# Window attention with expert routing on one core: keys loaded whole and spread by copies, ranking by half a comparison, and a tabled order of work

## The chip, the cores and the metric

The kernel runs on one core of one Trainium2 chip. The metric is the device time of one execution in microseconds (us). All inputs lie in HBM, in a layout that the host prepared, and the eight results (one for each batch entry) go back to HBM.

## What is computed

There are 8 batch entries, 8 heads, 576 positions and 64 features in a head. Heads 0 to 3 attend to a plain window of the last 32 positions; heads 4 to 7 attend to every fourth position of the last 128. The attention output of a batch entry, 576 rows of 512, is then the input of an expert layer, in which only the 128 rows with the highest gate score go through a two-layer network.

```python
scores = scale * np.matmul(q, k.transpose(0, 1, 3, 2))
scores = np.where(masks[None, :, :, :], scores, -1000000000.0)
scores = scores - np.max(scores, axis=-1, keepdims=True)
attn = np.exp(scores)
attn = attn / (np.sum(attn, axis=-1, keepdims=True) + 1e-09)
x = np.matmul(attn, v)            # then heads side by side: (B, S, 512)
...
scores = np.einsum('bsd,d->bs', x, w_gate)
for b in range(B):
    top_idx = np.argpartition(-scores[b], capacity)[:capacity]   # capacity = 128
    h = np.maximum(x[b, top_idx] @ w1, 0.0)                       # 512 -> 1024
    ye = h @ w2                                                   # 1024 -> 512
    g = 1.0 / (1.0 + np.exp(-scores[b, top_idx]))
    out[b, top_idx] = x[b, top_idx] + g[:, None] * ye
```

All of it is float32. The two products of the expert layer are made of three float32r products each (high part by high part, and the two mixed ones).

## The kernel before

**Units.** The attention of a batch entry is cut into five units: two of plain windows (`p`, 256 positions each), one of the last 64 positions of both kinds (`l`), and two of dilated windows (`d`). A unit goes through `scores` (line 275, TensorE; in the first `masked=20` units the mask is added by further products, line 270), `maximum` (line 287, VectorE; later units use line 294, which adds the mask and takes the maximum), `subtract` (line 303), `transposes` (line 314, TensorE), `weights` (line 342, exponentials on ScalarE), `attend` (line 356, TensorE), `normalise` (lines 369 and 371), `divide` (line 379 on VectorE, or line 385 on ScalarE), `store` (lines 394 to 404, DMAs on SyncE's queue) and `gate` (line 418, the gate score of each row). There are three score tiles in PSUM, one tile for `attend`, and three tiles `m` for everything else.

**Keys.** The score product takes two heads at once: 128 rows of the contraction hold the 64 features of two heads, and the key tile `ks` has two planes, in each of which the rows of the other head are zero. `load_k` (line 215) writes the keys of each half straight into its plane, so it issues two DMAs of 288 KB for each kind of window; `load_q` (line 208) issues one of 576 KB. There is one buffer for each kind: the next batch entry's keys may only be loaded when the scores that read the old ones are done. `load_vp` (line 221) loads rows 0 to 63 and 96 to 127 of a value table, in two DMAs; the exponentials of a `p` unit go to places in three pieces, and four tiles `pt` serve five units.

**Routing.** After the five units of an entry, `split_scores` (lines 450 to 453), `order` (lines 462 and 466, 15 small products), `total` (line 471), `spread` (line 477) and `gather_scores` (lines 483, 484) bring the scores of all 576 positions to every partition. `rank` (line 492) then compares each of five tiles of 128 positions with all 576 and counts; `mark` (line 499) makes a one-hot tile of the slots, `pick` (line 507) turns it into row numbers, `number` (line 513) makes them integers, and `fetch` (line 521) gathers the chosen rows from the result in HBM by an indirect DMA on GpSimd.

**Expert layer.** `gate_dot` (line 544) makes the gate score of the chosen rows anew, lines 549 to 554 the sigmoid, `turn_x` (line 559) turns the rows, `split_hi` and `split_lo` (lines 527, 530) split them, `ffn1` (line 598) and `ffn2` (line 624) are 24 products of 512 columns each, `result` (line 629) adds, and `put` (line 635) scatters the rows to HBM. The 16 weight blocks of 256 KB are loaded by `load_weights` (line 430), rounded on ScalarE (line 438), and their rests are made on GpSimd (line 442).

**What sets the order.** Nothing is written out by hand. Each step is an operation in `Planner`, with an engine, a cost, the operations that it needs, buffers that it takes and frees, and a due time. `run` simulates the engines: of the operations that could start within 0.05 us of the earliest on an engine, it takes the one with the lowest due time, plus a penalty when TensorE would change its tiling. The order found is the order in which the program issues. Every engine's queue is then worked strictly in that order. The planner takes DMAs to move `RATE = 0.29` KB per ns. SyncE issues each DMA as soon as its buffer is free, however many are under way. While TensorE would idle in the first 50 us, products on a spare tile fill the gap (line 837).

```python
first = min(t for t, _ in cands)
t, w = min((c for c in cands if c[0] <= first + 0.05),
           key=lambda c: (c[1].due + (self.penalty if c[1].mode not in (None, mode) else 0.0), c[1].n))
```

Of the kernel before, what the change touches and what calls it, by code (L numbers as in the profile page):

```python
# [19 lines left out]
P = 128  # L20
# [19 lines left out]
    unit=3,  # L40
    gate=14.47,
    unit0=2.82, gate0=5.68, route0=8.95, ffn0=17.53,
    route=13.4,
    ffn=14.64,
    piece=0.89,
    switch=3,
    w1=12.51, w2=25.55, each=2,
    first=4.62, early=15.02, lead=13.59,
# [3 lines left out]
    rest=16,  # L52
    split=(1, 2, 3, 4, 5, 6),
    aq=(),
    masked=20,
    xv=5,
    xe=20,
)


class Work:


    def __init__(self, n, eng, cost, fn, deps, due, mode, takes, frees, lag, size, after, port):
        self.n, self.eng, self.cost, self.fn, self.due, self.mode = n, eng, cost, fn, due, mode
        self.deps, self.takes, self.frees = [d for d in deps if d is not None], list(takes), list(frees)
        self.lag, self.size, self.after, self.port = lag, size, after, port
        self.start, self.end, self.fill = None, None, 0


class Planner:
# [4 lines left out]
    RATE = 0.29  # L76
    LAND = 2.0

    def __init__(self, bufs, switch, fill, free):
        self.ops, self.bufs, self.penalty, self.fill, self.free = [], bufs, switch, fill, dict(free)  # L80

    def add(self, eng, cost, fn, deps=(), due=0.0, mode=None, takes=(), frees=(), lag=0.0, size=None, after=0.0, port=False):
        w = Work(len(self.ops), eng, cost, fn, deps, due, mode, takes, frees, lag, size, after, port)
        self.ops.append(w)
        return w

    def run(self):
        users, left, ready, order = {}, {}, {}, []
        free, mode, moved, port = self.free, None, 0.0, {"DVE": 0.0, "POOL": 0.0}
# [14 lines left out]
        for _ in self.ops:  # L104
            best = None
            for eng, ws in ready.items():
                cands = []
                for t, w in ws:
                    t = max(t, free.get(eng, 0.0))
# [31 lines left out]
            if w.size is not None:  # L141
                moved = max(moved, t + 1.0) + w.size / self.RATE / 1000
                w.lag = max(w.lag, self.LAND, moved - w.end + 0.5)
# [21 lines left out]
def tile_window_attention_moe(ctx, tc, qt, kt, va, vb, w_gate, w1, w2, masks, mask_l, ident, slots, toks, outs, capacity):  # L165
# [8 lines left out]
    pl = Planner(dict(BUFS, **{f"oh{i}": 1 for i in range(nt)}), T["switch"], T["fill"], dict(PE=5.0, DVE=5.5, ACT=3.0, POOL=T["zeros"], SP=0.8))  # L174
# [9 lines left out]
    thr_sb = cp.tile([P, 2 * 512 + HB], F32, name="thr_sb")  # L184
    wg = cp.tile([P, DM], F32, name="wg")
    slots_sb = cp.tile([P, max(nt, 1) * P], F32, name="slots_sb")
    toks32 = cp.tile([P, NTOK], F32, name="toks32")
    toks_sb = cp.tile([P, NTOK], F16, name="toks_sb")
    qs = [cp.tile([P, 2, S + 16 * i], F32, name=f"qs{i}") for i in range(2)]
    ks = [cp.tile([P, 2, 2, G + S], F32, name=f"ks{i}") for i in range(2)]  # L190
    vp = cp.tile([3 * G, 8, VW], F32, name="vp")
    vd = cp.tile([P, 4, VW], F32, name="vd")
    vl = cp.tile([P, 3, VW], F32, name="vl")
    pts = [cp.tile([P, 4, 4, 2, G], F32, name=f"pt{i}") for i in range(4)]
# [7 lines left out]
    ohs = [cp.tile([P, NTOK, P], F16, name=f"oh{i}") for i in range(max(nt, 1))]  # L202
# [4 lines left out]
    def load_q(b, kind, lo=0, hi=S):  # L207
        nc.sync.dma_start(out=qs[kind][:, :, lo:hi], in_=qt[b, kind].rearrange("d (p s) -> d p s", p=2)[:, :, lo:hi])
# [10 lines left out]
    def load_vp(b, lo=0, hi=8):  # L219
        for k, src in ((slice(0, GK), slice(0, GK)), (slice(GK, 3 * G), slice(3 * G, P))):  # L220
            nc.sync.dma_start(out=vp[k, lo:hi].rearrange("k c f -> k (c f)"),
                              in_=va[b, src, (4 + lo) * VW:(4 + hi) * VW])

    def load_vd(b):
        nc.sync.dma_start(out=vd.rearrange("k r f -> k (r f)"), in_=va[b, :, 0:4 * VW])

    def load_vl(b):
        for i in range(2):
            nc.sync.dma_start(out=vl[GK * i:GK * i + LK, 0:2].rearrange("k e f -> k (e f)"),
                              in_=vb[b, LK * i:LK * (i + 1)])  # L230
        nc.sync.dma_start(out=vl[:, 2], in_=va[b, :, 12 * VW:13 * VW])
# [31 lines left out]
    def scores(g):  # L263
# [3 lines left out]
        for c, (nw, rows) in enumerate(chunks(kind)):  # L267
# [4 lines left out]
            for p in range(2):  # L272
                for w in range(nw):
                    q, q0, k, k0 = window(kind, s, c, w)
                    nc.tensor.matmul(st[G * w:G * (w + 1), c, p], q[:, p, q0:q0 + G], k[:, p, :, k0:k0 + GK],  # L275
# [32 lines left out]
    def transposes(g):  # L308
# [11 lines left out]
        ("p", 0): (((0, GK, 0),), ((G, G, 0), (GK, G, G))),  # L320
        ("l", 0): (((0, GK, 0),), ((GK, GK, 0),)),
        ("d", 0): (((3 * G, G, 0),), ((GK, GK, 0),)),
    }
    PLACES["p", 1] = PLACES["d", 1] = PLACES["p", 0]

    def held(g):
        b, u = divmod(g, NU)
        return pts[{0: b % 2, 1: 1 - b % 2, 2: 2, 3: 3, 4: b % 2}[u]]
# [17 lines left out]
    def attend(g):  # L346
# [3 lines left out]
        n = 3 * G if kind == "p" or (kind, s) == ("d", 1) else P  # L350
# [37 lines left out]
    def store(g):  # L388
# [3 lines left out]
        eng = nc.scalar if kind in T["aq"] else nc.sync  # L392
        if kind == "p":
            eng.dma_start(out=o[256 * s:256 * (s + 1), 0:256].rearrange("(c q) f -> q c f", c=2), in_=x)
        elif kind == "d":
            for r in range(2):
                for j in range(2 * s, 2 * s + 2):
                    i = HB * r + G * (3 - j if s else j)
                    eng.dma_start(out=o[P * j:P * (j + 1), 256:512].rearrange("(n c r) f -> r n c f", c=2, r=2)[r],
                                      in_=x[i:i + G])  # L400
        else:
            eng.dma_start(out=o[4 * P:S, 0:256], in_=x[0:HB, 1])
            for r in range(DIL):
                eng.dma_start(out=o[4 * P:S, 256:512].rearrange("(n r) f -> r n f", r=DIL)[r],
                                  in_=x[G * r:G * r + 16, 0])


    def gate(g):
        b, (kind, s) = g // NU, UNITS[g % NU]
        if b not in sts:  # L410
            sts[b] = {n: wk.tile([P, NTOK], F32, tag=n, name=f"{n}_{b}") for n in ("sd", "sc", "rk")}
            sts[b]["sw"] = sws[b % 2]
# [11 lines left out]
    def load_weights(i):  # L424
# [5 lines left out]
        nc.sync.dma_start(out=raw[i], in_=src)  # L430
# [13 lines left out]


    def split_scores(b, by_vector):
        st, eng = sts[b], nc.vector if by_vector else nc.gpsimd
        sp = st["sp"] = wk.tile([P, 3, NTOK], BF16, tag="sp", bufs=2, name=f"sp_{b}")
        rest = wk.tile([P, NTOK], F32, tag="rest", bufs=2, name=f"rest_{b}")
        eng.tensor_copy(sp[:, 0], st["sd"])  # L450
        eng.tensor_tensor(out=rest, in0=st["sd"], in1=sp[:, 0], op=ALU.subtract)
        eng.tensor_copy(sp[:, 1], rest)
        eng.tensor_tensor(out=sp[:, 2], in0=rest, in1=sp[:, 1], op=ALU.subtract)

    def order(b):
        st = sts[b]
        pg = st["pg"] = ps.tile([P, 512], F32, tag="m", bufs=BUFS["m"], name=f"pg_{b}")
        sp = st["sp"]
        for c in range(2):
            for e in range(2):  # L460
                for i in range(3):
                    nc.tensor.matmul(pg[:, c:4 - c:3 - 2 * c], perm[:, c, e],
                                     sp[:, i, 0:4].rearrange("q (s c) -> q c s", s=2)[:, e],
                                     start=e == 0 and i == 0, stop=e == 1 and i == 2)
        for i in range(3):
            nc.tensor.matmul(pg[:, 4:5], perml, sp[:, i, 4:5], start=i == 0, stop=i == 2)
# [450 lines left out]
```

## Time and profile before

| | us |
|---|---|
| median of 3 runs (lowest, highest) | 272.23 (271.6, 272.88) |
| the profiled execution's own time | 272.17 |
| its span, first to last instruction | 270.5 |
| TensorE busy | 240.9 (89%) |
| VectorE busy | 203.0 (75%) |
| ScalarE busy | 143.5 (53%) |
| GpSimd busy | 56.2 (21%) |
| bytes moved by DMA | 51.04 MB, mean 189 GB/s |

The profile is of one execution. "PE" is TensorE's products, "PEld" its weight loads, "DVE" VectorE, "ACT" ScalarE, "POOL" GpSimd, "SP" SyncE; "L275" is line 275. A group's row has the line, engine and operation, output and inputs with their shapes, the count, then the busy time in us and the mean of one in ns, then the idle time before them and what ended it. A row of the table of stretches has its bounds, its length, the busy time and count of each engine, TensorE's granted clock, the share of the 16 DMA engines and the GB/s. A row of the chain of waits has a start, a length and what it was.

### The profile page before, as it was taken

What the parts mean: (1) busy time and instruction counts of PE and PEld (TensorE: products, weight loads), DVE (VectorE), ACT (ScalarE), POOL (GpSimd) and SP (SyncE); (2) the same over time, 40 slices, a digit from 0 to 9 for tenths busy, and PEclk for the clock granted to TensorE, in tenths of its full rate; (3) what the DMA queues carried; (4) which work ended last, traced back from release to release, by engine and by line L of the source; (5) the groups of instructions that cost most, each with busy time, mean ns of one, the idle gap of its engine ahead of it and who ended that gap; (6) DMA issues with size and microseconds to landing.
All of it is one profiled execution on the core that took longest, in us unless ns stands there. A gap on an engine that the chain in (4) does not pass through costs nothing.

```text
span 270.5 us, 9035 instructions
## 1 busy us (share of the span) xinstructions
PE 240.9 (89%) x3469; PEld 194.0 (72%) x3475; DVE 203.0 (75%) x893; ACT 143.5 (53%) x418; POOL 56.2 (21%) x92
## 2 busy tenths in 40 slices
PE   6759859884997887999999999999999999999892
PEld 1439647673985875888888788788888878777671
DVE  4327885999597595999899989978899798684221
ACT  2062718328292255655585797578577948522120
POOL 8922103250430326101110111101110101011101
PEclk9997997999799799999999999999999999999998
DMA  6999984989879994998599689738994430321101
GB/s 157 257 238 255 284 242 102 299 210 247 240 175 249 239 302 123 315 282 180 150 252 283 194 256 303 219 83 219 286 230 122 138 120 21 88 69 42 39 0 39
DMA packets 28732, 51.04 MB, mean 189 GB/s; under 512 B 4529, under 2 KB 16049, under 8 KB 28017
## 3 DMA queue, kind: packets, MB, share of 16 engines
q1 hardware_dynamic: 26976, 46.16, 64.0%
q0 software_dynamic: 1280, 4.20, 4.7%
q8 instruction: 27, 0.44, 0.7%
q10 hardware_dynamic: 432, 0.11, 0.2%
q14 instruction: 17, 0.13, 0.2%
HBM read 38.92 MB, written 11.53 MB: 187 GB/s over the span
## 4 chain that ended last, share of the span: by engine, by line
PE 51%; DMA 13%; DVE 13%; issue 13%; SPq 5%; ACT 2%; POOL 1%; POOLq 1%; DVEq 0%; ACTq 0%
PE a L356 12%; PE py L624 10%; PE s L275 10%; DMA ks<-in_kt_dram 9%; PE ph L598 9%; PE s L314 5%; DMA raw<-in_w_dram 4%; DVE junk L492 3%; DVE junk L418 2%; DVE mx L287 2%; DVE ms L303 2%; DVE x L379 2%; PE pht L609 2%; ACT pt L342 2%; SPq L215 1%
## 5 line engine op out<-in xcount | busy, mean ns | idle before, releaser
L342 ACT ACTIVATE pt<-s 32x256 f32<-32x256 f32 (+2 forms) x208 | 76.8, 369 | 35.4 <-PE s L314 27.2
L275 PE MATMUL s<-ks,qs 128*32 128x128 f32 x1216 | 46.8, 288 | 7.1 <-DMA ks<-in_kt_dram 7.1
L275 PEld LDWEIGHTS s<-ks,qs 128*32 128x32 f32 x1216 | 38.5, 115 | 9.0 <-issue 5.8
L418 DVE CUSTOM_DVE_ANT_0 junk<-x,wg 128x256 bf16<-128x256 f32 x80 | 38.8, 486 | 5.7 <-ACT x L385 2.6
L492 DVE SCALAR_TENSOR_TENSOR junk<-sb,sc,thr_sb 128x576 bf16<-128x576 f32 (+1 forms) x40 | 32.4, 811 | 0.9 <-ACT sb L484 0.9
L385 ACT ACTIVATE x<-a,rin 128x64 f32<-128x64 f32 (+1 forms) x128 | 27.9, 328 | 9.7 <-DVE rin L371 6.3
L314 PE MATMUL s<-id,ms 128*128 128x128 f32 x160 | 25.0, 282 | 3.5 <-issue 2.7
L624 PE MATMUL py<-w2h,hh 128*128 128x512 f32 x64 | 27.4, 428 | 0.5 <-ACT w2h L438 0.5
L598 PE MATMUL ph<-w1h,xh 128*128 128x512 f32 x64 | 27.1, 424 | 0.7 <-ACT xh L527 0.7
L624 PE MATMUL py<-w2l,hh 128*128 128x512 f32 x64 | 25.4, 398 | 0.8 <-POOL w2l L442 0.8
L598 PE MATMUL ph<-w1h,xl 128*128 128x512 f32 x64 | 25.4, 397 | 0.0
L624 PE MATMUL py<-w2h,hl 128*128 128x512 f32 x64 | 25.3, 395 | 0.0
L598 PE MATMUL ph<-w1l,xh 128*128 128x512 f32 x64 | 25.2, 394 | 0.0
L314 PEld LDWEIGHTS s<-id,ms 128*128 128x128 f32 x160 | 18.3, 142 | 8.5 <-issue 3.6
L287 DVE TENSOR_REDUCE mx<-s 128x8 f32<-128x512 f32 (+2 forms) x24 | 13.9, 591 | 13.6 <-PE s L275 13.6
L294 DVE CUSTOM_DVE_ANT_0 ms<-s,mk 128x64 f32<-128x64 f32 (+1 forms) x144 | 22.2, 215 | 0.0
L356 PEld LDWEIGHTS a<-vp,pt 96*64 96x64 f32 x512 | 17.0, 142 | 6.5 <-ACT pt L342 4.6
L521 POOL DMA_INDIRECT xe<-out_dram,ix x8 | 7.9, 990 | 65.5 <-DMA vl<-in_va_dram 21.8
L356 PE MATMUL a<-vp,pt 96*64 96x65 f32 x512 | 19.3, 230 | 2.3 <-ACT pt L342 2.3
L356 PEld LDWEIGHTS a<-vd,pt 96*64 96x64 f32 (+1 forms) x512 | 16.3, 137 | 6.6 <-ACT pt L342 3.5
L356 PE MATMUL a<-vd,pt 96*64 96x65 f32 (+1 forms) x512 | 18.4, 224 | 2.3 <-ACT pt L342 1.2
L635 POOL DMA_INDIRECT out_dram<-y,ix x8 | 8.5, 1062 | 44.0 <-DVE y L629 19.9
(96 smaller groups left out, 398.0 us busy)
## 6 DMA issues: line engine op xcount, KB each, us to landing
qs<-in_qt_dram SPq DMA_DIRECT2D x15, 576.0 KB, 4.4
ks<-in_kt_dram SPq DMA_DIRECT2D x30, 288.0 KB, 9.8
out_dram<-x SPq DMA_DIRECT2D x72, 64.0 KB, 3.6
vd<-in_va_dram SPq DMA_DIRECT2D x8, 520.0 KB
raw<-in_w_dram SPq DMA_DIRECT2D x16, 256.0 KB, 3.8
out_dram<-x SPq DMA_DIRECT2D x16, 256.0 KB
vp<-in_va_dram SPq DMA_DIRECT2D x7, 520.0 KB, 11.3
vp<-in_va_dram SPq DMA_DIRECT2D x9, 260.0 KB
```

Source lines behind the costliest of these rows:

```text
L275: nc.tensor.matmul(st[G * w:G * (w + 1), c, p], q[:, p, q0:q0 + G], k[:, p, :, k0:k0 + GK], start=not by_products(g), stop=p == 1 or not b ...
L287: nc.vector.tensor_reduce(out=mx[:n, lo:hi].rearrange("q c p h -> q (c p h)"), in_=st[:n, lo:hi].rearrange("q c p h k -> q (c p h) k"), ax ...
L294: nc.vector.tensor_tensor_reduce(out=ms[:rows, c, p, h], in0=st[:rows, c, p, h], in1=mask_of(g, c)[:rows], scale=1.0, scalar=-3.0e38, op0= ...
L314: nc.tensor.transpose(tt[:, p, c], dt[:, c, p].rearrange("q h k -> q (h k)"), id32)
L342: nc.scalar.activation(held(g)[to:to + size, 2 * h:2 * h + 2, 0:n, u], src, AF.Exp, scale=SCALE)
L356: nc.tensor.matmul(at[HB * (y % 2):HB * (y % 2 + 1), c, f], held(g)[:n, h, y].rearrange("k u q -> k (u q)"), v[:n, f], start=True, stop=True)
L385: nc.scalar.activation(x[:n, c, h, :], av[:n, c, h, 0:D], AF.Copy, scale=rin[:n, c, h:h + 1])
L418: nc.vector.tensor_tensor_reduce(out=junk[:n], in0=x[:n, c].rearrange("q h d -> q (h d)"), in1=wg[:n, 256 * dil:256 * (dil + 1)], scale=UP ...
L492: nc.vector.scalar_tensor_tensor(out=junk[:n], in0=st["sb"][:n], scalar=st["sc"][:n, t:t + 1], in1=thr_sb[:n, o:o + S], op0=ALU.subtract, ...
L598: nc.tensor.matmul(e["ph", n], e[x][:, i, 0:P], w[:, i, n * 512:(n + 1) * 512], start=i == 0 and j == 0, stop=i == 3 and j == 2)
L624: nc.tensor.matmul(e["py", j], e[x][:, i, j * P:(j + 1) * P], w[:, i, :], start=i == 0 and n == 0, stop=i == 7 and n == 2)
L635: nc.gpsimd.indirect_dma_start(out=outs[b][:, :], out_offset=bass.IndirectOffsetOnAxis(ap=ix[:m, 0:1], axis=0), in_=e["y", j][:m], in_offs ...
```

## The change

**Keys.** `load_k` loads a kind's keys in one DMA of 576 KB into a new tile `kin`; `spread_k` copies each half to its plane of `ks`, with two ScalarE copies of 64 rows by 1152 columns. A new load of `kin` waits for the copies of the entry before; the copies wait for the scores that read the planes. `load_vp` loads all 128 rows in one DMA (1040 KB in place of about 780), the exponentials of a `p` unit are in two pieces, not three, and each of five units has a tile `pt` of its own.

**Ranking.** `rank` compares tile t only with the positions from its own on (576, 448, 320, 192 and 64 columns) and keeps the comparisons; `count` adds the missing ones by ten small products with a column of -1, and `ranks` joins both. `mark` is one operation of 640 columns. `order` has 5 products in place of 15, and `total` sums their three parts. `pick` also carries the three parts of each score (`split_sums`, on GpSimd), so that `number` has the chosen scores, and `gate_dot` is gone. The tables of slots and rows are made on GpSimd and no longer loaded.

**Transfers.** Every plain DMA goes through `move`. One on SyncE waits until the latest transfer that has at least 1200 KB issued behind it has landed. The planner models this and takes 370 KB per us.

**Order.** A table `RANKS` has one number for each operation. Where its length equals the number of operations, the numbers take the place of all due times, and the tiling penalty is zero. The due times' parameters change too; of these `w1`, `early` and `lead`, which bound when loads may start, still act, as do `masked=18`, `xv=2` and `xe=15` (which units mask by products and which divide on VectorE: 28 of 40 units in place of 24) and `rest=12` (four weight rests on VectorE).

```diff
-    def load_k(b, kind, lo=0, hi=S):
-        o = 0 if kind else G
-        src = kt[b, kind].rearrange("d (p s) -> d p s", p=2)
-        for h in range(2):
-            r = slice(h * D, (h + 1) * D)
-            nc.sync.dma_start(out=ks[kind][r, :, h, o + lo:o + hi], in_=src[r, :, lo:hi])
+    moves = []
+
+    def move(out, in_, kb, eng=None):
+        i = (eng or nc.sync).dma_start(out=out, in_=in_).ins
+        behind = 0
+        for j, size, calm in reversed(moves):
+            if eng is None and (behind >= T["under"] or calm):
+                tc.add_manual_dep(i, j.name, mybir.DependencyInfo(mybir.DependencyClass.Sync, mybir.DependencyReason.DATA),
+                                  reason="not too many transfers")
+                break
+            behind += size
+        moves.append((i, kb, False))
...
+    def load_k(b, kind):
+        move(kin[kind], kt[b, kind], 576)
+
+    def spread_k(b, kind, h, eng):
+        o, r = 0 if kind else G, slice(h * D, (h + 1) * D)
+        out = ks[kind][r, h, o:o + 2 * S]
+        eng.copy(out, kin[kind][r]) if eng is nc.scalar else eng.tensor_copy(out, kin[kind][r])
...
     def load_vp(b, lo=0, hi=8):
-        for k, src in ((slice(0, GK), slice(0, GK)), (slice(GK, 3 * G), slice(3 * G, P))):
-            nc.sync.dma_start(out=vp[k, lo:hi].rearrange("k c f -> k (c f)"),
-                              in_=va[b, src, (4 + lo) * VW:(4 + hi) * VW])
+        move(vp[:, lo:hi].rearrange("k c f -> k (c f)"), va[b, :, (4 + lo) * VW:(4 + hi) * VW], 130 * (hi - lo))
...
     def rank(b, t):
         st = sts[b]
-        n = P if t < 4 else HB
-        junk = wk.tile([P, S], BF16, tag="junk2", bufs=1, name=f"junk2_{b}_{t}")
-        o = 512 - t * P
+        n, o = P if t < 4 else HB, t * P
         nc.vector.scalar_tensor_tensor(
-            out=junk[:n], in0=st["sb"][:n], scalar=st["sc"][:n, t:t + 1], in1=thr_sb[:n, o:o + S],
+            out=cm[t][:n, 0:S - o], in0=st["sb"][:n, o:S], scalar=st["sc"][:n, t:t + 1], in1=thr_sb[:n, 0:S - o],
             op0=ALU.subtract, op1=ALU.is_gt, accum_out=st["rk"][:n, t:t + 1])
 
-    def mark(b, s, t):
+    def count(b):
+        pr = sts[b]["pr"] = ps.tile([P, 512], F32, tag="m", bufs=BUFS["m"], name=f"pr_{b}")
+        for t in range(1, NTOK):
+            for i in range(t):
+                nc.tensor.matmul(pr[:, t:t + 1], cm[i][:, (t - i) * P:(t - i + 1) * P], less, start=i == 0, stop=i == t - 1)
+
+    def ranks(b):
         st = sts[b]
-        n = P if t < 4 else HB
-        nc.vector.tensor_scalar(
-            out=ohs[s][:n, t, :], in0=slots_sb[:n, s * P:(s + 1) * P], scalar1=st["rk"][:n, t:t + 1],
-            scalar2=None, op0=ALU.is_equal)
+        rk = st["rk"][:, 1:NTOK]
+        nc.vector.tensor_tensor(out=rk, in0=st.pop("pr")[:, 1:NTOK], in1=rk, op=ALU.add)
+
+    def mark(b, s):
+        nc.vector.tensor_tensor(out=ohs[s], in0=slots_sb[:, s], in1=sts[b]["rk"].unsqueeze(2).to_broadcast([P, NTOK, P]),
+                                op=ALU.is_equal)
...
+    found = [int(r) for r in RANKS.split()]
+    if len(found) == len(pl.ops):
+        pl.penalty = 0.0
+        for w, r in zip(pl.ops, found):
+            w.due = r
     for i, w in enumerate(pl.run()):
```

More of the change, by code (lines that the diff above doesn't have):

```diff
@@ L39 @@
     warm=9,
[L40 to L48, printed above, removed]
+    unit=3.89,
+    gate=8.95,
+    unit0=1.86, gate0=-16.79, route0=8.14, ffn0=20,
+    route=1.69,
+    ffn=25.91,
+    piece=1.07,
+    switch=2.69,
+    w1=24.88, w2=34.11, each=0.86,
+    first=10, early=17.8, lead=15,
     fill=(50.0, 0.7),
@@ L51, with __init__ @@
     groups=(1,),
-    rest=16,
+    rest=12,
     split=(1, 2, 3, 4, 5, 6),
[L54 to L57, printed above, removed]
-)
+    spread=("ACT", "ACT"),
+    calm=(),
+    under=1200,
+    masked=18,
+    xv=2,
+    xe=15,
+)
+RANKS = """
[33 rows of a table added]
+"""
 class Work:
-    def __init__(self, n, eng, cost, fn, deps, due, mode, takes, frees, lag, size, after, port):
+    def __init__(self, n, eng, cost, fn, deps, due, mode, takes, frees, lag, size, after, port, calm):
         self.n, self.eng, self.cost, self.fn, self.due, self.mode = n, eng, cost, fn, due, mode
         self.deps, self.takes, self.frees = [d for d in deps if d is not None], list(takes), list(frees)
-        self.lag, self.size, self.after, self.port = lag, size, after, port
+        self.lag, self.size, self.after, self.port, self.calm = lag, size, after, port, calm
         self.start, self.end, self.fill = None, None, 0
@@ L88, in run @@
         users, left, ready, order = {}, {}, {}, []
-        free, mode, moved, port = self.free, None, 0.0, {"DVE": 0.0, "POOL": 0.0}
+        free, mode, moved, port, moves = self.free, None, 0.0, {"DVE": 0.0, "POOL": 0.0}, []
         pools = {t: [[0.0] * n, 0, {}] for t, n in self.bufs.items()}
@@ L104, in run @@
         for _ in self.ops:
-            best = None
+            best, under, clear = None, 0.0, 0.0
+            for size, end, calm in reversed(moves):
+                if under >= self.under or calm:
+                    clear = end
+                    break
+                under += size
             for eng, ws in ready.items():
@@ L173, in tile_window_attention_moe @@
     BUFS = dict(s=3, a=1, m=3, ms=3, x=4, xe=2 * nt + 2, raw=4, e=1)
-    pl = Planner(dict(BUFS, **{f"oh{i}": 1 for i in range(nt)}), T["switch"], T["fill"], dict(PE=5.0, DVE=5.5, ACT=3.0, POOL=T["zeros"], SP=0.8))
+    pl = Planner(dict(BUFS, **{f"oh{i}": 1 for i in range(nt)}), T["switch"], T["fill"], T["under"], dict(PE=5.0, DVE=5.5, ACT=3.0, POOL=T["zeros"], SP=0.8))
     id32 = cp.tile([P, P], F32, name="id32")
@@ L429, in load_weights @@
             src = w2[(i - 8) * P:(i - 7) * P, :]
-        nc.sync.dma_start(out=raw[i], in_=src)
+        move(raw[i], src, 256)
     def parts(i):
@@ new lines, in tile_window_attention_moe @@
+        o = ranked[b] = [A("DVE", 0.06 + 0.0013 * (S - P * t), lambda b=b, t=t: rank(b, t), [o] + counts[-1:], d + 1 + 0.5 * t, port=True) for t in range(NTOK)]
+        counts.append(A("PE", 0.3, lambda b=b: count(b), o, d + 4, mode=128, takes=[("m", ("pr", b))], lag=0.1))
+        o = A("DVE", 0.12, lambda b=b: ranks(b), counts[-1:] + ([picks[b - 2]] if b > 1 else []), d + 4, frees=[("m", ("pr", b))])
+        marks = [A("DVE", 0.75, lambda b=b, i=i: mark(b, i), [o], d + 4, port=True, takes=[(f"oh{i}", b)]) for i in range(nt)]
```

278 lines of the change are left out of this document (149 added, 129 removed), and 33 rows, old and new, of the table RANKS.

## The prediction

> **What bounds the kernel now.** I read the page's busy line first, then a table of stretches that I cut where the work changes its nature, and then the chain of waits inside the stretches that lose time.
>
> ```profile
> PE 240.9 (89%) x3469; PEld 194.0 (72%) x3475; DVE 203.0 (75%) x893; ACT 143.5 (53%) x418; POOL 56.2 (21%) x92
> GB/s 157 257 238 255 284 242 102 299 210 247 240 175 249 239 302 123 315 282 180 150 252 283 194 256 303 219 83 219 286 230 122 138 120 21 88 69 42 39 0 39
> ```
> ```profile
> 0.00:20.00 20.00, 12.25 (x158) 6.80 (x162) 7.17 (x16) 6.00 (x14) 13.80 (x35) 0.99 0.89 217
> 20.00:78.50 58.50, 48.94 (x966) 39.87 (x962) 47.76 (x139) 29.68 (x75) 16.26 (x17) 0.92 0.85 228
> 78.50:107.80 29.30, 24.60 (x327) 19.90 (x326) 21.39 (x65) 12.43 (x29) 7.89 (x9) 0.94 0.85 227
> 107.80:227.00 119.20, 118.90 (x1794) 99.00 (x1792) 108.03 (x616) 82.27 (x265) 13.41 (x27) 1.00 0.75 207
> 227.00:270.50 43.50, 36.24 (x241) 28.40 (x237) 18.70 (x59) 13.15 (x38) 4.87 (x5) 0.98 0.15 46
> ```
> ```profile
> 0.00:107.80 107.80, 85.79 (x1440) 66.58 (x1447) 76.31 (x219) 48.12 (x117) 37.95 (x61) 0.94 0.86 226
> ```
>
> From 107.8 to 227 us TensorE is busy 118.9 of 119.2 us at full clock: that stage is bound by TensorE, and nothing that is done for another engine there can shorten it. Before 107.8 us it is busy 85.8 of 107.8, at a clock of 0.94, and part of that busy time is spare products. In the same stretch the DMA engines are busy at 0.86 and move 226 GB/s. So the stage that can give something is the first one. The cut at 107.8 us is where the second entry's chosen rows are turned for its expert layer; the first entry's expert layer has just ended. The chain shows what that point waited for:
>
> ```profile
> 2.18 4.62 DMA ks<-in_kt_dram
> 9.92 9.38 DMA ks<-in_kt_dram
> 83.13 10.30 DMA ks<-in_kt_dram
> 93.49 8.20 DMA raw<-in_w_dram
> 102.55 2.63 DMA raw<-in_w_dram
> 105.89 1.28 POOL w2l L442
> 107.95 0.44 PE px L559 x4
> ```
> ```profile
> qs<-in_qt_dram SPq DMA_DIRECT2D x15, 576.0 KB, 4.4
> ks<-in_kt_dram SPq DMA_DIRECT2D x30, 288.0 KB, 9.8
> raw<-in_w_dram SPq DMA_DIRECT2D x16, 256.0 KB, 3.8
> ```
>
> Keys and weights stand in the chain for 4.62 + 9.38 + 10.30 + 8.20 + 2.63 = 35.1 us. A key transfer of 288 KB takes 9.8 us to land where a query transfer twice its size takes 4.4: it stands behind what was issued earlier and not needed as soon.
>
> **The change, stage by stage.** I count what must be done up to the same cut (the turning of the second entry's rows), for each resource that could set it, and take the rest of the program from the trace.
>
> *How much work lies before the cut.* I laid the tabled ranks over the operations: counting the operations of the new program by hand gives 962, as many as the table has, so the table is used. In that order the cut comes after the 15th attention unit (the fifth of the third entry). In the trace of before it comes after 16. The new program thus owes one more unit after the cut. Its price on TensorE:
>
> ```profile
> 158.14 1.88 PE s L275 x64
> 157.06 1.08 PE a L356 x32
> 154.38 0.59 PE s L314 x4
> 154.97 2.09 PE py L624 x9
> ```
>
> The first row is the scores of two units, 0.94 each; with 0.59 for the transposes and 1.08 for the attending products a unit is 2.61 us.
>
> *DMA up to the cut.* By the tabled order SyncE has issued, when the last weight block goes out: queries, keys and values of three entries (3 x 4190 KB), the gate row (256), queries and keys of one kind of the fourth entry (1152), 16 weight blocks (4096) and eleven units' results (2560). That is 20,634 KB, and with the first entry's gathered rows (256) 21.4 MB. At 226 GB/s this takes 94.7 us, at 226/0.86 = 263 (all engines busy) 81.4, and 1.5 us lie ahead of the first packet. The larger value table is in it (208 KB more for an entry, 0.6 MB here, 2.5 us at 250 GB/s). What speaks for a higher rate: fewer, whole transfers (the 30 key DMAs of the row above become 15), and keys that can be fetched while the planes are still read, because the new tile takes them; in before a key load sat behind the scores. I take 250 GB/s, 0.95 of the full rate: 85.6 + 1.5 = 87 us.
>
> *VectorE up to the cut.*
>
> ```profile
> L287 DVE TENSOR_REDUCE mx<-s 128x8 f32<-128x512 f32 x16 | 10.9, 680 | 7.1 <-PE s L275 7.1
> L303 DVE TENSOR_TENSOR ms<-s,mx 128x512 f32<-128x512 f32 x16 | 11.0, 690 | 2.1 <-POOL ms L715 1.5
> L369 DVE TENSOR_SCALAR den<-a 128x8 f32<-128x8 f32 x32 | 5.2, 161 | 9.5 <-PE a L356 8.9 <-PE pg L466 0.3
> L371 DVE RECIPROCAL rin<-den 128x8 f32<-128x8 f32 x32 | 6.5, 203 | 1.1
> L379 DVE TENSOR_TENSOR x<-a,rin 128x512 f32<-128x512 f32 x20 | 13.8, 689 | 1.0 <-DMA out_dram<-x 0.2
> L418 DVE CUSTOM_DVE_ANT_0 junk<-x,wg 128x256 bf16<-128x256 f32 x72 | 35.5, 493 | 5.2 <-ACT x L385 2.6 <-ACT h L604 0.2 <-ACT sb L484 0.2
> L492 DVE SCALAR_TENSOR_TENSOR junk<-sb,sc,thr_sb 128x576 bf16<-128x576 f32 x32 | 26.1, 814 | 0.9 <-ACT sb L484 0.9
> L499 DVE TENSOR_SCALAR oh<-slots_sb,rk 128x128 f16<-128x128 f32 x32 | 9.1, 285 | 1.1
> ```
>
> The L287 to L418 rows, the last of them twice, make 3.41 us for a unit; 15 units are 51.1. Routing an entry was 5 x (0.814 + 0.285) = 5.5. Now the comparisons have 1600 columns, not 2880: between 2.26 us (all by width) and 4.07 (nothing by width), and I take 2.5, near the first, as five rows of 576 columns are mostly width. The one marking operation of 640 columns is taken at 0.90, by width from the L492 row, and four further small ones at the L369 to L371 rows, 0.7. That is 4.1, so 1.4 us less for an entry, 8.2 for two. The first expert layer has four splits or sums and four weight rests at about 0.69 (the L379 row), 5.5. The sum is 65 us. It can start when the first scores are there, at about 11 us: 76 us if VectorE never waits. TensorE needs less: 15 x 2.61 + 48 x 0.232 (2.09/9) + some 4 for routing and masks = 54 us from 10 us on.
>
> *Start.* The first scores come later. Two whole transfers, 1.18 MB, must land (5.4 us at the 217 GB/s of the first row, from 1.5 on, and about 0.6 to signal: 7.5), and then two copies must run:
>
> ```profile
> L483 ACT COPY sb<-pa 128x512 f32<-128x512 f32 x8 | 4.7, 588 | 5.9 <-PE pa L477 5.9
> L484 ACT COPY sb<-pa 128x64 f32<-128x64 f32 x8 | 1.8, 221 | 0.0
> ```
>
> By these two rows a column is 0.82 ns, so 1152 columns cost 1.11 us; the bounds are 0.59 (the 512-column row) and 1.32 (that row by width alone). The first score is at 7.5 + 2.2 = 9.7 us, against 6.8 where the first key transfer ended. But the third unit, which needs both kinds, needs 2.89 MB in the new order of loads, 13.3 + 1.5 = 15 us, against 19.3 (9.92 + 9.38). So the stage starts 3 us later and is 4 us ahead after two units; the DMA term above already has this.
>
> *The cut and the end.* The cut moves from 107.8 to 87 by the largest of the three terms, DMA, 20.8 us. One unit is owed, 2.6. The stage behind the cut keeps its 162.7 us if nothing there becomes late: span 270.5 - 20.8 + 2.6 = 252.3. The execution's own time is 272.17 against a span of 270.5, 1.7 around it, and 272.17 is 0.06 below the median. Forecast: 254.0 us.
>
> *Does something become late behind the cut?* The rows for ScalarE and what leaves VectorE:
>
> ```profile
> L342 ACT ACTIVATE pt<-s 32x256 f32<-32x256 f32 x112 | 42.0, 375 | 4.2 <-PE s L314 1.8
> L385 ACT ACTIVATE x<-a,rin 128x64 f32<-128x64 f32 x112 | 24.8, 330 | 9.7 <-DVE rin L371 6.3 <-PE s L275 1.3 <-DMA out_dram<-x 1.0
> L544 DVE CUSTOM_DVE_ANT_0 junk<-xe,wg 128x512 bf16<-128x512 f32 x8 | 5.4, 680 | 1.7 <-DMA xe<-out_dram,ix 1.7
> L294 DVE CUSTOM_DVE_ANT_0 ms<-s,mk 128x64 f32<-128x64 f32 x128 | 19.6, 216 | 0.0
> L442 POOL TENSOR_TENSOR w2l<-raw,w2h 128x512 fp32r<-128x512 f32 x8 | 10.2, 1280 | 22.4 <-ACT w2h L438 22.3
> ```
>
> ScalarE gains 32 copies (35.5 us), loses two of six exponentials in each of 16 units (32 x 0.375 = 12.0) and four units' divisions (32 x 0.330 = 10.6): 143.5 + 13 = 156.5 us. Even if 10 us of that fell between 107.8 and 227, it would be 92 of 119. VectorE loses 8 x 1.4 for routing and 8 x 0.68 for the gate score, gains four divisions (2.8), four rests (2.7) and two units masked there (each 8 x 0.216 in place of 0.68, 1.0): about 9 us less. GpSimd loses four rests (5.1) and gains a split of four small operations for each entry. TensorE saves 10 of 15 small products and gains 10: nothing. With TensorE at 118.9 of 119.2, all this is covered there. The cover goes if a copy is late: it stands in ScalarE's queue ahead of a unit's exponentials, and TensorE's next attending product would wait, at 2.2 us for a pair.
>
> **The rivals.**
>
> *The same bytes at the same rate (chance 0.20).* The DMA engines were already busy at 0.86, and the change moves no byte less. Then the cut is at 94.7 + 1.5 = 96.2, the span 270.5 - 11.6 + 2.6 = 261.5, the time 263. For it: three stretches in a row with 217 to 228 GB/s, whatever was computed. Against it: slices at 284 to 315, so the mean is not the ceiling.
>
> *VectorE is the bound (0.20).* If bytes arrive in time throughout, the cut is at 76 and the time 270.5 - 31.8 + 2.6 + 1.7 = 243. Against it: in the 20-to-78.5 row VectorE is busy only 47.8 of 58.5.
>
> *The hold on transfers starves the core: slower (0.10).* SyncE now waits until an earlier transfer has landed, and everything behind stands in its queue: results, which the gathers wait for, and the next loads. The price can be worked out. All loads (37,872 KB) and the results of about seven entries (8064), 47.0 MB, must have moved some 43 us before the end (the last entry's units end there in the trace, the 227.00 row). So 273.6 us, the edge of "slower", asks for 47.0/(273.6 - 1.7 - 43) = 205 GB/s; below that the kernel is slower. With 1.23 MB under way this is a landing time of 6.0 us. At 186 GB/s (6.6 us) the time would be 253 + 43 + 1.7 = 298. The query row, 576 KB in 4.4 us amid other transfers, speaks against it; the key row, 9.8, speaks for it, but that is backlog which the hold itself removes. [...]
>
> *The plan does not fit the chip: no change (0.05).* Every queue is worked in the planned order, and the planner now takes 370 KB per us. The best slice of the page is 315 GB/s. Where a product is queued ahead of one whose data is there, its wait comes back; if the 20.8 us come back that way, the time is near 272. [...]
>
> **How the numbers follow.** The forecast has 0.45. Rivals: 0.20 at 263, 0.20 at 243, 0.10 slower, 0.05 no change. About 0.5% (1.4 us) is what can be told from no change, so faster 0.85, same 0.05, slower 0.10. The range goes from 243 (VectorE) to 267 (the first rival and one more late unit and copy, 2.6 + 1.5); it leaves out the slower case, the unchanged one and a little below.
>
> **What would show it.** First scores near 9.7 us and the third unit's near 15; the second entry's rows turned near 87 us, 15 units before it; DMA near 250 GB/s up to there; TensorE without gaps behind; key transfers gone from the chain but for the first; 32 copies near 1.1 us. The sum is wrong if that turn is not early, or if it is early and the stage behind it is longer than 165 us.

## The result and the profile after

The kernel after took 260.5 us (257.65 to 260.88, 4 runs) against 272.12 us (271.6 to 272.88, 4 runs) before: a ratio of 0.955, with a 95% interval of 0.948 to 0.962. The forecast was 254.0 us with a range of 243 to 267, so the time lies inside the range, but the gain is 11.6 us where 18.1 were forecast. The profiled execution took 260.74 us, with a span of 259.0. The times of the runs are medians of all executions, while the ratios leave out those that took over 1.5% longer than their kernel's fastest; the profiles of two experiments below, the column halves and the hold of 600 KB, are of such slow executions.

The busy line, the GB/s of the 40 slices and the packets of the page:

```profile
PE 236.3 (91%) x3442; PEld 186.4 (72%) x3442; DVE 194.3 (75%) x918; ACT 160.9 (62%) x386; POOL 60.9 (24%) x149
...
GB/s 209 339 329 346 309 151 283 345 324 199 314 214 353 272 232 361 206 259 232 124 273 230 191 257 322 168 157 197 273 127 177 72 17 101 73 39 40 43 0 40
DMA packets 24571, 53.10 MB, mean 205 GB/s; under 512 B 3920, under 2 KB 14288, under 8 KB 23632
```

More bytes are moved (53.1 against 51.0 MB), and the slices of the first third now lie mostly between 280 and 360 GB/s, where before they lay around 240. The table of stretches, cut at the same event as in the prediction (the turning of the second entry's rows, line 635 here, at 85.64 us) and at the last attending product (222.2 us; before it was at 231.5):

```profile
0.00:85.60 85.60, 74.15 (x1318) 55.74 (x1319) 69.15 (x207) 56.48 (x112) 36.89 (x91) 1.00 0.87 287
...
85.60:222.20 136.60, 133.65 (x1955) 109.00 (x1954) 112.26 (x674) 97.67 (x261) 19.20 (x50) 1.00 0.64 199
222.20:259.00 36.80, 28.53 (x174) 21.61 (x173) 12.91 (x39) 6.70 (x13) 4.82 (x8) 0.99 0.12 38
```
```profile
107.80:231.50 123.70, 123.40 (x1844) 102.59 (x1842) 110.80 (x629) 86.68 (x280) 14.38 (x28) 1.00 0.74 203
231.50:270.50 39.00, 31.74 (x190) 24.80 (x189) 15.93 (x47) 8.74 (x23) 3.91 (x4) 0.98 0.13 41
```

The second fence is the kernel before, cut at the same events. Up to the cut 22.2 us were gained (107.8 to 85.6). Behind it 10.7 us were given back (162.7 to 173.4): the middle stretch grew from 123.7 to 136.6 us, and TensorE, idle there for 0.3 us before, is now idle for 3 us. The DMA engines are as busy before the cut as they were (0.87, was 0.86) and move 287 GB/s in place of 226: the same busy share carries a quarter more bytes in each us.

Rows of the chain of waits around the cut, and two rows of the timeline, the first scores and those of the third unit:

```profile
64.23 4.63 DMA raw<-in_w_dram
...
74.31 3.92 DMA raw<-in_w_dram
78.25 8.02 DMA kin<-in_kt_dram
86.35 1.16 ACT ks L280
87.52 1.16 ACT ks L280
...
109.61 6.33 DMA qs<-in_qt_dram
```
```profile
7.46 0.65 PE L337 MATMUL s<-ks,qs 128*32 128x128 f32 x16
...
12.65 0.64 PE L337 MATMUL s<-ks,qs 128*32 128x128 f32 x16 [1.29 <-ACT pt L404]
```

Key loads have not left the chain, but only one is in it: it takes 8.02 us from 78.25 on, its two copies run just after the cut, and a query load stands at 109.6. TensorE's waits behind the cut, grouped by what released them, are these (columns: total us, times, longest):

```profile
PE pg L529 <- DVE sp L508: 1.7, 1, 1.7
PE s L337 <- DMA qs<-in_qt_dram: 1.2, 1, 1.2
PE s L337 <- ACT ks L280: 1.2, 1, 1.2
```

### The profile page after: what moved, and what is told of

It is laid out like the page before. It is cut to its first block, busy times and chain, and to the rows that moved or that the text cites. A ratio compares the mean times of both kernels' runs of the same rounds, so it can differ in the third digit from the quotient of the medians.

```text
span 259.0 us, 9004 instructions
## 1 busy us (share of the span) xinstructions
PE 236.3 (91%) x3442; PEld 186.4 (72%) x3442; DVE 194.3 (75%) x918; ACT 160.9 (62%) x386; POOL 60.9 (24%) x149
## 4 chain that ended last, share of the span: by engine, by line
PE 45%; DMA 14%; issue 11%; DVE 6%; POOL 3%; ACT 3%; SPq 2%; POOLq 1%; DVEq 0%; ACTq 0%
PE ph L674 11%; PE a L418 10%; PE py L700 9%; PE s L337 7%; DMA raw<-in_w_dram 6%; PE s L377 4%; DMA kin<-in_kt_dram 3%; DMA out_dram<-x 3%; DMA qs<-in_qt_dram 2%; SPq L257 2%; PE pht L685 2%; DVE ms L357 2%; ACT ks L280 2%; PE pa L544 1%; POOL w1l L501 1%
## 5 line engine op out<-in xcount | busy, mean ns | idle before, releaser
L404 ACT ACTIVATE pt<-s 64x256 f32<-64x256 f32 (+2 forms) x176 | 64.6, 367 | 23.6 <-PE s L377 16.7
L337 PE MATMUL s<-ks,qs 128*32 128x128 f32 x1216 | 43.5, 274 | 7.2 <-ACT ks L280 2.7
L280 ACT COPY ks<-kin 64x1152 f32<-64x1152 f32 x32 | 36.9, 1153 | 17.3 <-DMA kin<-in_kt_dram 11.8
L337 PEld LDWEIGHTS s<-ks,qs 128*32 128x32 f32 x1216 | 35.1, 109 | 10.0 <-ACT ks L280 4.3
L477 DVE CUSTOM_DVE_ANT_0 junk<-x,wg 128x256 bf16<-128x256 f32 x80 | 37.2, 465 | 3.1
L357 DVE CUSTOM_DVE_ANT_0 ms<-s,mk 128x64 f32<-128x64 f32 (+1 forms) x160 | 24.6, 216 | 2.8 <-PE s L337 2.7
L447 ACT ACTIVATE x<-a,rin 128x64 f32<-128x64 f32 (+1 forms) x96 | 20.9, 328 | 8.0 <-DVE rin L433 4.0
L559 DVE SCALAR_TENSOR_TENSOR cm<-sb,sc,thr_sb 128x576 bf16<-128x576 f32 (+4 forms) x40 | 19.5, 540 | 2.0 <-ACT sb L551 2.0
L441 DVE TENSOR_TENSOR x<-a,rin 128x512 f32<-128x512 f32 (+2 forms) x34 | 19.6, 592 | 1.3 <-DMA out_dram<-x 0.5
L418 PE MATMUL a<-vp,pt 128*64 128x65 f32 x512 | 18.6, 224 | 0.0
```

The lines of the kernel that those rows point to most:

```text
L280: eng.copy(out, kin[kind][r]) if eng is nc.scalar else eng.tensor_copy(out, kin[kind][r])
L337: nc.tensor.matmul(st[G * w:G * (w + 1), c, p], q[:, p * S + q0:p * S + q0 + G], k[:, :, p * S + k0:p * S + k0 + GK], start=not by_product ...
L357: nc.vector.tensor_tensor_reduce(out=ms[:rows, c, p, h], in0=st[:rows, c, p, h], in1=mask_of(g, c)[:rows], scale=1.0, scalar=-3.0e38, op0= ...
L404: nc.scalar.activation(held(g)[to:to + size, 2 * h:2 * h + 2, 0:n, u], src, AF.Exp, scale=SCALE)
L418: nc.tensor.matmul(at[HB * (y % 2):HB * (y % 2 + 1), c, f], held(g)[:n, h, y].rearrange("k u q -> k (u q)"), v[:n, f], start=True, stop=True)
L441: nc.vector.tensor_tensor(out=x[:n, lo:hi], in0=av[:n, lo:hi, :, 0:D], in1=rin[:n, lo:hi].unsqueeze(3).to_broadcast([n, hi - lo, 4, D]), o ...
```

## The experiments

Every kernel but one is the kernel after with the edits named. Those of a group ran on one chip, beside the kernel before (medians 272.96, 272.36 and 270.45 us in the three groups). Four things could have brought the gain: the form of the transfers (whole keys move their bytes faster); the copies and the tile `kin`, which let keys be fetched while the planes are still read; the tabled order; or the halved ranking. For the 6.5 us that were missing from the gain, the hold on transfers was the first suspect.

### One part undone

**The order by due times.** The table is left aside, and the planner orders by due times and penalty, as the kernel before does.

```diff
-    found = [int(r) for r in RANKS.split()]
+    found = []
```

> The changed kernel with the table of ranks ignored, so that the due times and the tiling penalty set the order; everything else as changed. If the gain comes from transfers that arrive sooner (first theory), most of it stays: 262 to 266 us, the second entry's rows turned at 86 to 92 us. If the tabled order brings it (rival), the time goes back to 268 to 273 and the turn to 95 us or later.

262.87 us (259.23 to 264.84), ratio 0.957 [0.948, 0.967]; the cut at 85.45 us. The ratio of the kernel after is 0.955, so with the hold in place the tabled order brings nothing that the intervals show.

**No hold.** `move` never waits for an older transfer.

```diff
-            if eng is None and (behind >= T["under"] or calm):
+            if eng is None and (behind >= 1000000 or calm):
```

> The changed kernel with the same order of issue, but no transfer waits for an earlier one to land. If the hold on transfers is what lets the needed bytes arrive first (rival), the turn of the second entry's rows goes from 85.6 us to above 92 and the time to 266 or more. If the order of issue and whole transfers do it (first theory), the time stays within 2 us of 260.5 us, and waits of the SyncE queue for transfers go away.

254.49 us (252.87 to 255.52), ratio 0.935 [0.929, 0.941]. This is below both kernels, and neither expected answer came. The stretches:

```profile
0.00:84.20 84.20, 73.08 (x1313) 55.67 (x1319) 70.18 (x207) 57.60 (x113) 36.43 (x91) 1.00 0.87 299
84.20:253.00 168.80, 160.86 (x2126) 130.33 (x2124) 124.98 (x712) 103.30 (x274) 24.03 (x58) 1.00 0.52 166
```

The cut moves only 1.4 us, but the stage behind it is 4.6 us shorter (173.4 to 168.8), with the same 2126 products. The kernel after was measured in another group, but the two ratios to the kernel before, 0.935 [0.929, 0.941] and 0.955 [0.948, 0.962], lie apart. The hold costs where the prediction thought that all was covered.

**Two sets of key planes.** Keys go straight into planes in 64-row transfers, but into a set for even and one for odd entries, so that they too can be fetched early; there are no copies. To make room the thresholds of `rank` are bfloat16 and the spare products' tile is smaller, and GpSimd clears two more planes. The edit of `load_k`:

```diff
-        move(kin[kind], kt[b, kind], 576)
+        o = 0 if kind else G
+        for h in range(2):
+            r = slice(h * D, (h + 1) * D)
+            move(ks[kind][b % 2][r, h, o:o + 2 * S], kt[b, kind][r], 288)
```

> The changed kernel with two sets of key planes, into which the keys are loaded directly, each half of 64 rows by a DMA of its own, with no copies on ScalarE; same order. If whole transfers of 128 rows are what raised the rate from 226 to 287 GB/s up to the turn (first theory), the rate falls below 265 and the time rises to 263 or more, although 37 us of copies are gone. If the copies cost more than the whole transfers bring (rival), the waits of TensorE for ScalarE's copies (2.7 us) go and the time falls to 256 to 259.

275.63 us (271.63 to 276.81), ratio 1.006 [0.994, 1.018]: the whole gain is gone. The cut is at 95.35 us, and queries keep TensorE waiting:

```profile
0.00:95.35 95.35, 78.46 (x1313) 60.48 (x1319) 69.24 (x207) 40.84 (x98) 41.88 (x99) 0.91 0.88 257
```
```profile
PE s L337 <- DMA qs<-in_qt_dram: 12.6, 4, 4.3
```

Fetching early isn't enough for the gain. The DMA engines are busy at 0.88 and move 257 GB/s.

**Ranking over all columns.** `rank` compares with all 576 positions again, and the column of -1 is zero, so that `count` adds nothing. The tiles are widened to fit.

```diff
...
-            out=cm[t][:n, 0:S - o], in0=st["sb"][:n, o:S], scalar=st["sc"][:n, t:t + 1], in1=thr_sb[:n, 0:S - o],
+            out=cm[t][:n, 0:S], in0=st["sb"][:n], scalar=st["sc"][:n, t:t + 1], in1=thr_sb[:n, 512 - o:512 - o + S],
...
-        nc.gpsimd.memset(less, -1.0)
+        nc.gpsimd.memset(less, 0.0)
```

> The changed kernel with each tile of scores compared with all 576 positions again, as before; the counting products stay, with a column of zeros. VectorE has about 1.7 us more work for each entry, 13 in all. If VectorE is covered, as the prediction says of the stage behind the cut, the time rises by less than 1.5 us. If VectorE's chain sets the pace before the cut (rival), two entries' 3.4 us come back there and the last entry's 1.7 at the end: 264 to 266 us.

262.1 us (260.95 to 263.27), ratio 0.964 [0.957, 0.970]. The ranking's group, first in this kernel and then in the kernel after:

```profile
L559 DVE SCALAR_TENSOR_TENSOR cm<-sb,sc,thr_sb 128x576 bf16<-128x576 f32 (+1 forms) x40 | 31.2, 832 | 2.0 <-ACT sb L551 2.0
```
```profile
L559 DVE SCALAR_TENSOR_TENSOR cm<-sb,sc,thr_sb 128x576 bf16<-128x576 f32 (+4 forms) x40 | 19.5, 540 | 2.0 <-ACT sb L551 2.0
...
L280 ACT COPY ks<-kin 64x1152 f32<-64x1152 f32 x32 | 36.9, 1153 | 17.3 <-DMA kin<-in_kt_dram 11.8
```

The ranking is 11.7 us longer and VectorE in all 8.2 (202.5 us against 194.3); the kernel is longer by some 2 us, and the intervals overlap. That is between the two expected answers. The third row answers to the forecast of 1.11 us for a copy.

### The form of the key transfers

The next two keep the tile, the copies, the hold and the table, and cut each key transfer in two of 288 KB: by rows (64 partitions, 4608 bytes each) or by columns (128 partitions, 2304 bytes each).

```diff
-        move(kin[kind], kt[b, kind], 576)
+        for h in range(2):
+            move(kin[kind][h * D:(h + 1) * D], kt[b, kind][h * D:(h + 1) * D], 288)
```
```diff
-        move(kin[kind], kt[b, kind], 576)
+        for h in range(2):
+            move(kin[kind][:, h * S:(h + 1) * S], kt[b, kind][:, h * S:(h + 1) * S], 288)
```

> The changed kernel with each key load cut into two DMAs of 64 rows by 4608 bytes; the copies, the order and the hold stay. If transfers of 64 rows are what is slow (first theory, after the run with two sets of planes came out at 1.006 of the kernel before), the rate up to the turn of the second entry's rows falls from 287 to below 270 GB/s and the time rises to 266 us or more. If the slowness of that run came from its longer set-up on GpSimd or its missing copies (rival), the time stays within 2 us of 260.5.

> The changed kernel with each key load cut into two DMAs of 128 rows by 2304 bytes: as many DMAs, of the same size, as in the run with halves of 64 rows. If the number of rows decides (first theory), the time stays within 2 us of 260.5. If the number of DMAs or the shorter rows decide (rival), it rises as in the run with halves of 64 rows.

Row halves: 274.53 us (272.43 to 278.94, 10 runs), ratio 1.007 [1.001, 1.012]. Column halves: 264.92 us (262.01 to 266.67), ratio 0.968 [0.957, 0.978]. The row halves up to their cut:

```profile
0.00:96.45 96.45, 78.58 (x1313) 60.30 (x1319) 68.12 (x207) 56.55 (x112) 36.73 (x91) 0.91 0.86 255
```

By the ratios, twice as many transfers of half the size cost some 3 or 4 us, more than the 2 that were expected, though this interval overlaps that of the kernel after; when each of them writes only 64 partitions, the rest of the gain goes as well.

**The forms by themselves.** A kernel that only moves inputs, one form after the other, twice round; VectorE reads one column of each tile as it lands.

> This kernel computes nothing of the reference: it only loads keys, queries and values in several forms, each phase after the one before has landed, twice over: four whole transfers of 128 rows by 4608 bytes; eight of 64 rows by 4608; eight of 128 rows by 2304; eight of 64 rows by twice 2304 bytes into planes; two value tables of 128 rows by 8320; the same as four of 64 rows. If the number of rows decides, the phases of 64 rows move their 2.36 MB (2.13 MB of values) at least 20% slower than those of 128 rows, with the 128 by 2304 form like the whole one. If the length of the rows decides, the two forms of 2304 bytes are the slow ones. If neither does, all phases have the same rate within 5%.

Rows of VectorE's timeline, first round: a row's first number is the time just after a landing. From the first pair to the last: whole keys, row halves, column halves (of queries, which have the same size), the value table whole, the value table in two halves of 64 rows.

```profile
4.55 0.15 DVE L190 COPY seen<-whole 128x1 f32<-128x1 f32 x1 [3.63 <-DMA whole<-in_kt_dram]
...
8.99 0.15 DVE L190 COPY seen<-whole 128x1 f32<-128x1 f32 x1 [1.26 <-DMA whole<-in_kt_dram]
14.28 0.15 DVE L190 COPY seen<-rows 128x1 f32<-128x1 f32 x1 [5.14 <-DMA rows<-in_kt_dram]
...
21.77 0.15 DVE L190 COPY seen<-rows 128x1 f32<-128x1 f32 x1 [2.25 <-DMA rows<-in_kt_dram]
...
25.57 0.15 DVE L190 COPY seen<-cols 128x1 f32<-128x1 f32 x1 [0.54 <-DMA cols<-in_qt_dram]
...
31.37 0.15 DVE L190 COPY seen<-cols 128x1 f32<-128x1 f32 x1 [0.56 <-DMA cols<-in_qt_dram]
...
49.31 0.15 DVE L190 COPY seen<-vwhole 128x1 f32<-128x1 f32 x1 [5.18 <-DMA vwhole<-in_va_dram]
51.77 0.15 DVE L190 COPY seen<-vwhole 128x1 f32<-128x1 f32 x1 [2.30 <-DMA vwhole<-in_va_dram]
59.80 0.15 DVE L190 COPY seen<-vsplit 128x1 f32<-128x1 f32 x1 [7.88 <-DMA vsplit<-in_va_dram]
64.14 0.15 DVE L190 COPY seen<-vsplit 128x1 f32<-128x1 f32 x1 [4.18 <-DMA vsplit<-in_va_dram]
```

Three whole key loads of 589,824 bytes land in 8.99 - 4.55 = 4.44 us, 1.48 each: 399 GB/s. Three pairs of row halves, with the same bytes, take 21.77 - 14.28 = 7.49 us, 2.50 each: 236 GB/s. The value table (1,064,960 bytes) comes at 433 GB/s whole (2.46 us) and at 245 in halves (4.34 us). In the second round the same four come to 398, 229, 421 and 232 GB/s. Nothing else ran, so it is the form. That there are two transfers in place of one explains only a part: three pairs of column halves take 31.37 - 25.57 = 5.80 us, 305 GB/s, and 385 in the second round. So they are not quite like whole keys, as had been expected of them, but clearly faster than row halves.

### The size of the hold, and halves without it

Four kernels on one chip: the hold at 2400 KB and at 600 KB in place of 1200, no hold again, and row halves without a hold (the edits of the row halves and of "no hold" together).

```diff
-            if eng is None and (behind >= T["under"] or calm):
+            if eng is None and (behind >= 600 or calm):
```

> The hold lets 2400 KB be under way in place of 1200. With the hold a TensorE idle of 5.9 us behind the cut and a median of 260.5 us were measured, without it 2.4 us and 254.5 us. Theory A (the hold costs because SyncE's queue stands still until an older transfer lands, and so the transfers behind it start late): a looser hold costs less, 255 to 257 us. Theory B (the hold's cost comes from the waits as such, one more for each DMA, whatever the bytes): as many waits remain, 260 us.

> The hold lets only 600 KB be under way in place of 1200. Theory A (late starts): more than 5 us longer than with 1200 KB, 266 us or more, with a lower rate before the cut. Theory B (the waits as such): 260 us, as with 1200 KB.

> The kernel without the hold once more, so that it stands beside the other two sizes on one chip: 254.5 us as measured before, 253 to 256, if its lead over the kernel after is real; 260 us if that lead was one chip's.

> Keys in two transfers of 64 rows each, as in the experiment with row halves, and no hold. With the hold these halves cost 14 us over whole keys (274.5 against 260.5). Theory A (the 64-row form itself moves its bytes slowly, about 240 GB/s against about 400): the loss stays without the hold, 10 to 14 us over 254.5, so 264 to 269 us. Theory B (the loss came from the hold, which with slower transfers stands still for longer): most of it goes, 255 to 259 us.

| kernel | median us (lowest, highest) | ratio to before |
|---|---|---|
| hold 600 KB | 274.42 (271.08, 275.52) | 1.014 [1.004, 1.024] |
| hold 2400 KB | 256.43 (254.83, 257.41) | 0.950 [0.942, 0.958] |
| no hold | 253.81 (252.61, 255.42) | 0.943 [0.934, 0.951] |
| row halves, no hold | 272.33 (270.09, 273.5) | 1.012 [1.005, 1.020] |

Each up to its own cut, in the order of the table:

```profile
0.00:95.10 95.10, 76.61 (x1313) 58.42 (x1319) 69.74 (x207) 56.77 (x112) 36.87 (x91) 0.95 0.78 252
```
```profile
0.00:85.99 85.99, 75.14 (x1314) 57.46 (x1319) 68.36 (x207) 56.92 (x113) 36.65 (x91) 0.96 0.85 289
```
```profile
0.00:82.59 82.59, 72.84 (x1313) 56.63 (x1319) 68.20 (x207) 56.95 (x113) 35.81 (x91) 0.98 0.88 301
```
```profile
0.00:93.60 93.60, 78.08 (x1314) 60.42 (x1320) 67.24 (x207) 56.65 (x112) 36.11 (x91) 0.93 0.87 262
```

The first and the last row look alike in length and GB/s, and the share beside the GB/s tells them apart. Under the tight hold the engines are busy at 0.78: they are starved. With row halves they are busy at 0.87, close to the 0.88 without a hold, and still move 262 against 301 GB/s: each byte costs more of their time. The halves lose 11.0 us up to the cut; eight key loads are issued by then (a ninth goes out just ahead of the cut), and at 2.50 - 1.48 = 1.02 us more each they make an estimated 8.2 us of the 11. They lose 5.4 more behind it (its span is 268.4 us, that without a hold 252.0, so 174.8 against 169.4). The whole loss, 18.5 us, is more than the 10 to 14 that were expected.

The hold's price runs with its size, as theory A has it. The kernel with 1200 KB was measured in another group, and its ratio, 0.955, lies near that of 2400; the intervals of these two overlap, and so do those of 2400 and of no hold beside it. Only the 600 KB lie clearly apart. With 600 KB TensorE's waits behind the cut are

```profile
PE s L337 <- DMA qs<-in_qt_dram: 4.7, 1, 4.7
PE s L337 <- ACT ks L280: 1.9, 1, 1.9
```

where the kernel after had 1.2 and 1.2 in the same two rows; without a hold the first is gone and the second is 0.2 at most.

**No hold and no table.** The edits of the first two experiments together (it ran beside the row halves).

> The changed kernel without the hold on transfers and without the table of ranks. With due times alone the kernel took 262.9 us, without the hold 254.5. If the two act apart (first theory), this takes 255 to 258. If the order found by due times needs the hold, because it issues later loads earlier (rival), it takes 262 or more.

260.93 us (258.21 to 261.34), ratio 0.953 [0.944, 0.963], against 0.935 and 0.943 for the two runs with the table and without the hold. So without the hold the tabled order is worth some 3 to 5 us by the ratios, of which only the larger is clear of the intervals, and with it nothing that shows. Neither expected answer came (255 to 258, or 262 and more). The planner still reckoned with a hold of 1200 KB when it made this order, so the order was not made for a free queue. A part of the loss can be read in the waits: with the order by due times TensorE's expert products wait 2.1 us behind the cut for ScalarE's copies `sb` of the gate scores, with the hold and without, and with the table they do not. The rest was not followed.

## Why the prediction was right or wrong

**The direction and the place: right.** Only the first stage could give much, and it did: the cut was forecast at 87 us and came at 85.6, with 15 attention units ahead of it.

**The DMA term: near in its number by luck, wrong in its working.** It took 21.4 MB at 250 GB/s. What moved up to the cut was 287 GB/s x 85.6 us = 24.6 MB: the count stopped at the last weight block, and by the cut SyncE had issued nine key loads where seven were counted. Too few bytes and too low a rate made up for each other. And 226/0.86 = 263 GB/s was taken for the rate with all engines busy. It was only the rate of that mixture of forms; the busy share stayed and the rate rose to 287, and to 301 without the hold. Of the two reasons given for a higher rate, "fewer, whole transfers" carries the gain (the row halves undo it, alone); "keys that can be fetched while the planes are still read" shows none by itself, since the row halves and the two sets of planes keep it and end at before's time. The value table, too, was loaded by 96 rows before and by 128 after; no run undoes that alone. What was missing is the number of partitions that a transfer writes: the bare keys came at 399 GB/s with 128 and at 236 with 64. The trace of before had a hint of it, the 288 KB key rows landing in 9.8 us beside 4.4 for twice the bytes, which the prediction put down to backlog alone.

**The first rival, the same rate for the same bytes (263 us):** its time was near, by other steps. Its cut (96.2) did not come; the row halves had it (96.45, and 93.6 without the hold).

**VectorE as the bound (243):** did not come; it was busy for 69 of 85.6 us (65 were forecast). With the ranking 11.7 us dearer, the kernel is some 2 us longer.

**The hold starves the core (0.10, slower):** the mechanism was there. At 1200 KB it cost some 3 to 5 us (ratios 0.955 against 0.943 and 0.935, each in its own group), at 600 KB all of the gain and more. It did not decide, as the first-stage gain was larger. The prediction asked only for a mean rate (205 GB/s, with 287 measured up to the cut) and so looked for its price where bytes are short. The price was behind the cut, in single loads issued too late: the waits for `qs` and `ks` above. The rival's edge is 1.23 MB landing in 6.0 us; on SyncE's queue the bare whole keys, four issued together (2.36 MB), landed after a median of 5.4 us.

**The plan does not fit the chip:** the tabled order did not lose (0.955, and 0.957 by due times), though the best slice, 361 GB/s where it was 315 before, is still under the plan's 370 KB per us.

**What failed: "The stage behind the cut keeps its 162.7 us if nothing there becomes late", with 2.6 us for the one unit owed.** It became 173.4, 10.7 more; that and the cut, 1.4 us early, make the 6.7 us between the forecast and the profiled execution (8.1 - 1.4). The prediction had named this as a sign that its sum is wrong, a stage longer than 165 us; its own 162.7 + 2.6 already touched that limit. The busy time of the scores (first row), the attending products and the expert layer's first products (last row) behind the cut, before and then after:

```profile
107.80:270.50 162.70, 21.10 (x640) 17.60 (x640) 0.99 0.59 164
107.80:270.50 162.70, 27.61 (x728) 24.32 (x728) 0.99 0.59 164
107.80:270.50 162.70, 43.95 (x168) 30.11 (x168) 0.99 0.59 164
```
```profile
85.60:259.00 173.40, 23.58 (x696) 19.60 (x696) 1.00 0.53 165
85.60:259.00 173.40, 28.98 (x760) 25.52 (x760) 1.00 0.53 165
85.60:259.00 173.40, 46.53 (x168) 29.26 (x168) 1.00 0.53 165
```

There are 32 attending products more, the one unit that was counted (1.4 us); but 56 score products more, since the old order had run ahead with scores by nearly one more unit (2.5 us, where the prediction had 0.94). With 8 more transposes (some 0.6 us, counted from the start of one product to the start of the next) the debt is about 4.4 us, not 2.6. TensorE's idle time behind the cut, summed over its timeline, rose by 3.9 us (1.95 to 5.89); without the hold it was 2.4 and 2.6. The rest, some 2 us, is mainly the same number of expert products taking longer (43.95 to 46.53 in the last rows): the new order cuts them into more pieces, 26 against 18, between products of another shape. That the cutting is the cause is not shown: the order by due times has 29 pieces, and they take 46.77 us, hardly more than the 26.

**The cover.** The copies cost 1153 ns where 1.11 us were forecast, ScalarE was at 160.9 us (156.5 forecast) and VectorE lost 8.7 us (9). The prediction's "The cover goes if a copy is late" happened once, at 86.35 us in the chain, where two copies (2.3 us) follow a key load that was issued only when a weight block had landed, at 78.25. But what waited was the next score product, 1.2 us, and not an attending product.

**The start.** Better than forecast: first scores at 7.46 us (9.7), the third unit's at 12.65 (15). The 217 GB/s used for the first loads were a mean over a mixture with 64-row forms; now the first two loads, whole, are there earlier. Two small terms of the start had no row beside them: 1.5 us ahead of the first packet, where the first packet of the loads starts at 2.27 us in the kernel before and at 1.85 us in the kernel after, and 0.6 to signal, where the first keys of the kernel before landed at 6.80 us, 0.67 us after the last of their packets.

## What to carry to other kernels

A DMA busy share near 0.87 says that the engines are occupied, not that the rate is a ceiling (here 226 GB/s stood beside 0.86 and 301 beside 0.88): look at the form of each transfer first, and spread it over all 128 partitions (bare keys: 399 GB/s, and 236 over 64) even if a copy on an engine with spare time must then put the data in place. When a stage is shortened, count everything that the old order had already done ahead of the cut, each kind of product by itself, and look behind the cut for the loads that a limit on transfers makes late. Here a limit on bytes under way was best left out: the kernel with the change and without the hold, 253.8 and 254.5 us, is the fastest of all that were run.

## What the runs showed of the hardware that had not been expected

With nothing else running, transfers on SyncE's queue reached 398 to 433 GB/s when each wrote 128 partitions whole, 305 to 385 as column halves, and 229 to 245 when each wrote 64 partitions. The best slice of the kernel before had 315. TensorE's granted clock up to the cut was 0.94 before, 1.00 after, and 0.91 to 0.93 in the kernels with 64-row keys; whether the lower clock added to their loss was not separated. It did not simply follow TensorE's share of busy time: it was 1.00 at 74.15 of 85.6 us in the kernel after, and 0.96 at 75.14 of 85.99 with the hold of 2400 KB.
